# Two token tiles turned on TensorE, two tiles' statistics on ScalarE, and a held weight load

## The chip, the core and the metric

The kernel runs on one core of a Trainium2 chip. The core's engines work side by side and wait for each other through semaphores: TensorE (PE in the profile: matmuls, and its weight loads as PEld), ScalarE (ACT), VectorE (DVE), GpSimd (POOL) and SyncE (SP), which here only issues DMA transfers. The metric is the time of one execution on the device in microseconds (us), smaller is better; the median of three runs before is 1055.08 us (1054.37 to 1055.83).

## The reference

A transformer block with attention and a gated channel MLP, on 2048 tokens of width 1024 in bf16. Normalized tokens `xn` feed both branches:

```python
xn = layernorm(x)                               # x: 1 x 2048 x 1024
# attention, 32 heads of width 32
q, k, v = split(xn @ wqkv)
s = softmax(q @ k.T * 32**-0.5) @ v @ wo
# MLP with its own layernorm, F = 3584
h = gelu(layernorm(xn) @ w1 + b1)
g = silu(h @ w2 + b2)
out = x + s * g
```

(The layout of heads is left out here.) Softmax needs 32 x 2048 x 2048 exponentials, all on ScalarE.

## The kernel before

The kernel is a program that builds a list of operations with their engine, an assumed cost, and what they read and write, lets its own list scheduler (`plan.run`) choose the order for every engine by those assumed costs, and then emits the instructions in that order, with semaphore waits. On the chip each engine runs its list strictly in order. So a changed assumption about a cost moves instructions, though it computes nothing different.

A token tile is 128 tokens x 1024. There are 16 (t = 0 to 15); two of them are a pair n. The opening of the kernel does the following for each tile: load it, take mean and variance, compute the reciprocal root on GpSimd, normalize to bf16 on VectorE (`xnb`, four buffers), turn it so that the width lies on partitions (`xnT`, in `big`), and project K, V and part of Q from it. Tiles below `TD` are turned on TensorE (transposes into PSUM, copied out by ScalarE), the others by a DMA transpose issued from SyncE. Tiles in `AS` have their statistics taken by ScalarE in two passes with an accumulator, the others by VectorE.

```python
XF = 4; QE = 0; AS = (2,); TD = 2; XA = 8; XB = 5; XW = 9
...
for t in range(XF): load_x(t)                   # order of the first loads
wk0 = load_qk(0, 1)
wq0 = load_qk(0, 0)
for t in range(XF, 6): load_x(t)
load_v(0)                                       # wv
for t in range(6, XA): load_x(t)
...
for n in range(NPR):                            # pairs
    for t in (2 * n, 2 * n + 1):
        if t in AS:                             # statistics on ScalarE
            act(activation(junk, xst[t], Copy, scale=-1/32768, accum_out=lnp[:, t, 2:3]))
            act(activation(junk, xst[t], Square, bias=lnp[:, t, 2:3], scale=1/32, accum_out=mv[:, t, 1:2]))
            dve(tensor_scalar_mul(mv[:, t, 0:1], lnp[:, t, 2:3], -32.0))
        else:                                   # statistics on VectorE
            for c in range(2): dve(bn_stats(stats[:, t, c, :], xst[t][:, c * 512:(c + 1) * 512]))
            dve(bn_aggr(mv[:, t, :], stats[:, t]))
        for k in range(XA, NT):                 # later tiles are loaded behind these statistics
            if max(0, k - XB) == t: load_x(k, [("st", t, 0)])
    ...                                         # reciprocal root on GpSimd, then
    xnop[t] = dve(tensor_scalar(xnb[t % 4], xst[t], mean, rstd, subtract, mult))
    for t in (lo, lo + 1):
        if t < TD:
            pro_q.append(tr_item(t))            # 8 TensorE transposes, copy out on ScalarE
        else:
            add("SP", dma_start_transpose(out=xnT[:, :, tile t], in_=xnb[t % 4]), ...)
    pro_q.append(k_pair_item(n, False))         # K of the pair, 8 matmuls of 256
    if n == 1: pro_q.append(q_pair_item(1))     # Q of pair 1
    if n >= VLAG: pro_q.append(v_item(0, n - VLAG, "pro"))   # V, 16 matmuls of 256
```

(Helper arguments, costs and the two tiles of pair 0, which are handled one by one, are cut.) Attention then goes through units: four heads, 256 queries (block qb), 256 keys (pair kp). A unit is eight small score matmuls (two halves of four) and two exponentials of 128 x 1024 on ScalarE, one for each half (line 1181), later the product of the probabilities with V ("PV") on TensorE. The first units alternate between query blocks 0 and 1: (0,0), (0,1), (1,0), (1,1), (0,2), (1,2), (0,3), (1,3) and so on up to pair 7. Units of pair kp can start when K of that pair exists, that is when both its tiles are turned. The exps of this opening are counted from 1 here: 1 and 2 belong to (0,0), 3 and 4 to (0,1), 9 to 12 to the units of pair 2, 13 to 16 to pair 3, 17 to 20 to pair 4, 21 to 24 to pair 5, 25 to 28 to pair 6; 29 is the first of pair 7. While TensorE has nothing to do in the first 32 us of its schedule, "fillers" (matmuls of the identity) are put in.

The weights of the MLP are loaded ahead: `w1` in pieces of 256 KB, the first three pairs of pieces held behind a normalized tile, and `w2` in pieces of 448 KB, not held:

```python
def load_w1(p):
    ...
    dma(f"w1{gi}{i}", ..., [xnop[XW + 2 * p]] if p < 3 else [])
def load_w2(q, r):
    ...
    dma(f"w2{i}", lambda e: e.dma_start(w2r[:, i], src), 580000, [], [("w2", i)])
```

Of the kernel before, what the change touches and what calls it, by code (L numbers as in the profile page):

```python
# [34 lines left out]
XF = 4  # L35
# [5 lines left out]
WLAT = 3300  # L41
# [1 line left out]
NCUT = 2  # L43
HALF = 1
NU = 22
QE = 0
AS = (2,)
FILL = 300
ADJ2 = 0
TD = 2  # L50
XA = 8
XB = 5
XW = 9
ENGS = ("PE", "ACT", "DVE", "POOL", "SP")


# [18 lines left out]
class _Plan:  # L75
# [54 lines left out]
    def run(self, total_units, dense_slack):  # L130
# [28 lines left out]
        def commit(o, t):  # L159
            e = o.eng  # L160
            o.start = t
            if e == "SP":
                if o.prio >= 5:
                    for x in reversed(order["PE"]):
                        if x.fin <= t:
                            o.deps[x] = True
                            break
                tf[e] = t + o.occ
                state["bw"] = max(state["bw"], t) + o.nbytes / 380.0
                o.fin = state["bw"] + {"w1": WLAT, "w2": WLAT, "tp": 2800.0, "x0": 2050.0, "x1": 2000.0, "x2": 2500.0}.get(o.sem[:2], 2300.0)  # L170
            else:
                tf[e] = t + o.occ
                o.fin = t + o.occ + o.lat
            order[e].append(o)
            self.seq.append(o)
            release(o, t)
            wake(tf[e], e)
# [267 lines left out]
        while ev:  # L445
            t, ei = heapq.heappop(ev)
            e = ENGS[ei]
# [109 lines left out]
def bass_recurrent_scan__mha_block__mixer_channel_mlp__prompt_kernel(  # L557
# [39 lines left out]
    with ExitStack() as st:  # L597
# [112 lines left out]
        def pool(fn, occ, R, W, prio=3):  # L710
            return add("POOL", fn, occ, PL, R, W, prio)

        def dma(sem, fn, nbytes, R, W, prio=3, extra=()):
            return add("SP", fn, 430, 0, R, W, prio, sem=sem, nbytes=nbytes, extra=extra)

        def chunk(item, fn, occ, R, mode="f", W=()):
            o = add("PE", lambda e, fn=fn, item=item: fn(e, item.bank), occ, TL, R, W, item=item, mode=mode)
# [36 lines left out]
        def load_v(pr):  # L754
            src = A_wqkv[:, 2 * D + pr * 256: 2 * D + (pr + 1) * 256].rearrange("(c p) n -> p c n", p=128)
            dma("wv", lambda e: e.dma_start(wv, src), 850000, [], [("wv",)])
# [2 lines left out]
            load_x(t)  # L759
        wk0 = load_qk(0, 1)  # L760
        wq0 = load_qk(0, 0)
        for t in range(XF, 6):
            load_x(t)
        load_v(0)
        for t in range(6, XA):
            load_x(t)
        pool(lambda e: e.iota(iota_i, pattern=[[1, 128]], base=0, channel_multiplier=-1), 300, [], [("iota",)])
        dve(lambda e: e.tensor_single_scalar(ident[:], iota_i, 0, op=ALU.is_equal), 220, [("iota",)], [("ident",)], 0)
        dve(lambda e: e.memset(ones[:], 1.0), 90, [], [("ones",)], 0)
# [114 lines left out]
        for n in range(NPR):  # L884
            for t in (2 * n, 2 * n + 1):
                if t in AS:

                    junk = yT[:, 4:8, :].rearrange("p c t -> p (c t)")
                    act(lambda e, t=t: e.activation(junk, xst[t], ACT.Copy, scale=-1.0 / 32768, accum_out=lnp[:, t, 2:3]),
                        c_acts(1024) + 93, [XS(t)], [("yT", 2), ("yT", 3), ("st", t, 0)], 1)  # L890
                    act(lambda e, t=t: e.activation(junk, xst[t], ACT.Square, bias=lnp[:, t, 2:3], scale=1.0 / 32,
                                                    accum_out=mv[:, t, 1:2]),
                        c_acts(1024) + 186, [XS(t), ("st", t, 0)], [("yT", 2), ("yT", 3), ("st", t, 1)], 1)
                    dve(lambda e, t=t: e.tensor_scalar_mul(mv[:, t, 0:1], lnp[:, t, 2:3], -32.0), 65,
                        [("st", t, 0), ("st", t, 1)], [("mv", t)], 1)
                else:
                    for c in range(2):
                        dve(lambda e, t=t, c=c: e.bn_stats(stats[:, t, c, :], xst[t][:, c * 512:(c + 1) * 512]),  # L898
                            600, [XS(t)], [("st", t, c)], 1)
                    dve(lambda e, t=t: e.bn_aggr(mv[:, t, :], stats[:, t, :, :].rearrange("p c s -> p (c s)")),  # L900
                        150, [("st", t, 0), ("st", t, 1)], [("mv", t)], 1)
                for k in range(XA, NT):
                    if max(0, k - XB) == t:
                        load_x(k, [("st", t, 0)])
            lo, hi = 2 * n, 2 * n + 2
            if n == 0:
                for t in (0, 1):
                    dve(lambda e, t=t: e.tensor_scalar_add(lnp[:, t:t + 1, 0], mv[:, t:t + 1, 1], EPS), 90, [("mv", t)], [("ve", 0, t)], 0)
                    pool(lambda e, t=t: e.tensor_tensor(lnp[:, t:t + 1, 1], lnp[:, t:t + 1, 0], mhalf[:, t:t + 1], op=ALU.pow),
                         650, [("ve", 0, t), ("mhalf",)], [("rs", 0, t), ("rs", 0)], 0)  # L910
                    dve(lambda e, t=t: e.tensor_scalar(xnb[t], xst[t], mv[:, t, 0:1], lnp[:, t, 1:2],
                                                       op0=ALU.subtract, op1=ALU.mult), 455,
                        [XS(t), ("mv", t), ("rs", 0, t)], [("xnb", t)], 0.5)
                pro_q += [tr_item(0), qk_tile_item(0), tr_item(1, 0), tr_item(1, 1), qk_tile_item(1)]
                if VLAG == 0:
                    pro_q.append(v_item(0, 0, "pro"))
                continue
            dve(lambda e, lo=lo, hi=hi: e.tensor_scalar_add(lnp[:, lo:hi, 0], mv[:, lo:hi, 1], EPS), 90,
                [("mv", lo), ("mv", lo + 1)], [("ve", n)], 1)
            dve(lambda e, lo=lo, hi=hi: e.tensor_scalar_mul(lnp[:, lo:hi, 4], mv[:, lo:hi, 0], -1.0), 65,  # L920
                [("mv", lo), ("mv", lo + 1)], [("nm", n)], 1)
            pool(lambda e, lo=lo, hi=hi: e.tensor_tensor(lnp[:, lo:hi, 1], lnp[:, lo:hi, 0], mhalf[:, lo:hi], op=ALU.pow),
                 700, [("ve", n), ("mhalf",)], [("rs", n)], 0)
            pool(lambda e, lo=lo, hi=hi: e.tensor_tensor(lnp[:, lo:hi, 5], lnp[:, lo:hi, 4], lnp[:, lo:hi, 1], op=ALU.mult),
                 200, [("nm", n), ("rs", n)], [("nb_", n)], 0)
            for t in (lo, lo + 1):
                if t in DN:
                    xnop[t] = dve(lambda e, t=t: e.tensor_scalar(xnb[t % 4], xst[t], mv[:, t, 0:1], lnp[:, t, 1:2],
                                                                 op0=ALU.subtract, op1=ALU.mult), 455,
                                  [XS(t), ("mv", t), ("rs", n)], [("xnb", t % 4)], 0.5)  # L930
                    continue
                xnop[t] = pool(lambda e, t=t: e.tensor_scalar(xnb[t % 4], xst[t], lnp[:, t, 1:2], lnp[:, t, 5:6],
                                                    op0=ALU.mult, op1=ALU.add), 950,
                     [XS(t), ("nb_", n), ("rs", n)], [("xnb", t % 4)], 1)
            for t in (lo, lo + 1):
                if t < TD:
                    pro_q.append(tr_item(t))
                else:

                    add("SP", lambda e, t=t: e.dma_start_transpose(out=xnT[:, :, t * 128:(t + 1) * 128], in_=xnb[t % 4]),  # L940
                        1290, 0, [("xnb", t % 4)], [("xnT", t, h) for h in range(2)], 0, sem=f"tp{t % 4}", nbytes=262144)
            pro_q.append(k_pair_item(n, False))
            if n == 1:
                pro_q.append(q_pair_item(1))
            if n >= VLAG:
                pro_q.append(v_item(0, n - VLAG, "pro"))
        for n in range(NPR - VLAG, NPR):
            pro_q.append(v_item(0, n, "pro"))
        q_at = len(pro_q)

        pool(lambda e: e.tensor_tensor(lnp[:, :, 2], mv[:, :, 1], lnp[:, :, 1], op=ALU.mult), 150,
             [("rs", n) for n in range(NPR)], [("s2",)], 2)
# [22 lines left out]
        def load_w1(p):  # L975
            gi = p % NW1R
            pi = p % NW1
            for i in range(2):
                src = B_w1[i * 512:(i + 1) * 512, pi * 256:(pi + 1) * 256].rearrange("(c p) f -> p c f", p=128)
                dma(f"w1{gi}{i}", lambda e, i=i, src=src: e.dma_start(w1r[gi][:, 4 * i:4 * i + 4], src), 332000, [], [("w1", gi, i)], 3,  # L980
                    [xnop[XW + 2 * p]] if p < 3 else [])

        def load_w2(q, r):
            i = nw2["n"] % NW2R
            nw2["n"] += 1
            src = B_w2[r * 7 * 128:(r + 1) * 7 * 128, q * 256:(q + 1) * 256].rearrange("(f p) n -> p f n", p=128)
            dma(f"w2{i}", lambda e: e.dma_start(w2r[:, i], src), 580000, [], [("w2", i)])
            return i

        def b1_item():  # L990
# [349 lines left out]

        for tq in range(1, 4):
            it = qk_item(0, 0, tq, wq0, 16 * tq - 12)
            if tq == 1 and QE:
                it.kind, it.due = "pro", 1
                pro_q.insert(q_at - QE, it)
                continue
            plan.queues["proj"].append(it)
            it.after = 1000
# [144 lines left out]
```

The softmax here doesn't subtract the row's maximum and nothing guards it: scores larger than these inputs give would overflow.

## Time and profile before

| | before |
|---|---|
| median of 3 runs | 1055.08 us |
| span of the profiled execution | 1055.5 us |
| TensorE busy | 1028.4 us (97%) |
| ScalarE busy | 1013.0 us (96%) |
| VectorE busy | 960.5 us (91%) |
| exps, 128 x 1024 | 1024, 964.8 us busy |
| DMA transposes | 14 |

A line of the profile's timeline gives start and length in us, the engine, the line of the source, the operation, what it writes and reads, a count of merged instructions, and in brackets how long the engine had been idle before and what ended that. A "q" behind an engine's name is its instruction queue; a DMA is issued there, and its data land later. `gw` and `yT` are the buffers of normalized tiles, `big` the turned tokens, `hT` and `w2r` the raw token tiles before they become hidden values and weights, `qk` projections and their weights, `ut` statistics, `P` probabilities, `ps` PSUM. The chain of waits follows the last instruction back, at each step to what released it.

### The profile page before, as it was taken

The page shows a single profiled execution, that of the slowest core. Times are in us where ns is not written, and L with a number is a line of the kernel's source. Part 1 is how long each engine was busy: PE and PEld are TensorE (multiplying, and loading weights), DVE is VectorE, ACT ScalarE, POOL GpSimd, SP SyncE. Part 2 cuts the span into 40 slices and gives each one's busy share as a digit, 9 for nine tenths or more (in the row PEclk, how much of TensorE's full clock was granted, in tenths as well). Part 3 has the DMA queues.
Part 4 walks back from the last instruction along what each step waited for, and adds up shares of the span by engine and source line. Part 5 has one row for each costly group of instructions (what it writes and reads, how often), then busy time and mean ns, then how long its engine had stood idle before and what let it go on. Part 6 is the DMA issues. An engine that isn't in the chain of part 4 may idle for free.

```text
span 1055.5 us, 32143 instructions
## 1 busy us (share of the span) xinstructions
PE 1028.4 (97%) x14326; PEld 637.6 (60%) x14326; DVE 960.5 (91%) x1454; ACT 1013.0 (96%) x1104; POOL 14.8 (1%) x28
## 2 busy tenths in 40 slices
PE   8899999999999999999999999999999999999997
PEld 4445566656676566656676566656665667664442
DVE  7659999999899999999999999999989999979897
ACT  4699999999999999999999999999999999999993
POOL 1200000000000000000000000000000000000000
PEclk9999999999999999999999999999999999999999
DMA  9945256743276356634465456434475587673431
GB/s 234 186 111 148 79 161 191 197 127 96 70 221 173 108 148 185 173 109 113 117 189 161 113 164 183 141 104 116 143 198 161 171 236 221 205 221 95 137 102 60
DMA packets 302371, 160.16 MB, mean 152 GB/s; under 512 B 40218, under 2 KB 293146, under 8 KB 302234
## 3 DMA queue, kind: packets, MB, share of 16 engines
q1 hardware_dynamic: 302234, 158.12, 53.8%
q8 instruction: 112, 1.84, 0.7%
q14 instruction: 25, 0.20, 0.1%
HBM read 142.35 MB, written 12.06 MB: 146 GB/s over the span
## 4 chain that ended last, share of the span: by engine, by line
ACT 85%; PE 11%; DMA 2%; DVE 1%; SPq 0%; issue 0%; DVEq 0%
ACT P L1181 79%; PE ps L728 7%; ACT ut L1042 5%; PE ps L723 2%; PE ps L1167 2%; ACT gw L1078 1%; DMA big<-gw 1%; DMA big<-yT 1%; DMA hT<-in_A_x_dram 0%; DVE w1r L1328 0%; DVE ut L898 0%; SPq L742 0%; PE ps L866 0%; DVE V L1331 0%; DVE V L1328 0%
## 5 line engine op out<-in xcount | busy, mean ns | idle before, releaser
L1181 ACT ACTIVATE P<-ps 128x1024 bf16<-128x1024 f32 x1024 | 964.8, 1241 | 20.3 <-PE ps L1167 20.2
L1211 DVE TENSOR_TENSOR PA<-P 128x2048 bf16<-128x2048 bf16 x245 | 297.7, 1217 | 17.8 <-ACT P L1181 16.5
L728 PE MATMUL ps<-yT,w1r 128*128 128x256 bf16 x1792 | 232.5, 273 | 0.6 <-DVE yT L1010 0.6
L728 PE MATMUL ps<-w2r,hT 128*128 128x256 bf16 x1792 | 225.0, 273 | 1.8 <-DVE xb L1027 0.6
L728 PEld LDWEIGHTS ps<-yT,w1r 128*128 128x128 bf16 x1792 | 162.7, 98 | 56.2 <-issue 30.6
L728 PEld LDWEIGHTS ps<-w2r,hT 128*128 128x128 bf16 x1792 | 163.8, 98 | 50.8 <-issue 29.6
L723 PE MATMUL ps<-P,V 128*32 128x256 bf16 x4096 | 144.7, 274 | 1.2 <-DVE xb L1027 0.7
L728 PE MATMUL ps<-big,qk 128*128 128x512 bf16 (+2 forms) x568 | 133.4, 361 | 6.1 <-DMA big<-gw 3.8
L1216 DVE TENSOR_TENSOR PA<-PA 128x1024 bf16<-128x1024 bf16 x201 | 135.6, 681 | 1.2
L728 PE MATMUL ps<-qk,big 128*128 128x256 bf16 (+1 forms) x736 | 128.0, 308 | 0.9 <-DMA qk<-in_A_wqkv_dram 0.8
L723 PEld LDWEIGHTS ps<-P,V 128*32 128x32 bf16 x4096 | 97.2, 96 | 34.2 <-issue 23.6
L1167 PE MATMUL ps<-qk 32*128 32x256 bf16 x2048 | 108.6, 274 | 6.0 <-ACT P L1181 5.4
L1167 PE MATMUL ps<-QKT 32*128 32x256 bf16 x2048 | 101.7, 273 | 1.4 <-ACT P L1181 1.2
L728 PEld LDWEIGHTS ps<-qk,big 128*128 128x128 bf16 x736 | 65.2, 98 | 44.8 <-issue 19.2
L1027 DVE TENSOR_TENSOR xb<-ps,b1T 128x512 bf16<-128x512 f32 x112 | 76.4, 684 | 8.4 <-PE ps L728 7.1
L728 PEld LDWEIGHTS ps<-big,qk 128*128 128x128 bf16 x568 | 47.8, 98 | 57.4 <-issue 17.3
L1167 PEld LDWEIGHTS ps<-qk 32*128 32x128 bf16 x2048 | 32.2, 92 | 75.6 <-ACT P L1181 69.0
L1167 PEld LDWEIGHTS ps<-QKT 32*128 32x128 bf16 x2048 | 30.3, 92 | 70.9 <-ACT P L1181 67.8
L1042 ACT ACTIVATE ut<-ut 128x1024 f32<-128x1024 f32 x56 | 71.8, 1282 | 0.0
L1045 DVE SCALAR_TENSOR_TENSOR hT<-ut,xb 128x1024 bf16<-128x1024 f32 x56 | 67.9, 1212 | 1.3 <-ACT ut L1042 0.8
L1040 DVE SCALAR_TENSOR_TENSOR ut<-hT,xb 128x1024 f32<-128x1024 bf16 x56 | 67.9, 1215 | 0.0
L1261 DVE STREAM_TRANSPOSE nt<-ps 128x256 f32<-128x256 f32 x64 | 28.6, 446 | 22.8 <-PE ps L723 22.6
(82 smaller groups left out, 539.6 us busy)
## 6 DMA issues: line engine op xcount, KB each, us to landing
w1r<-in_B_w_dram SPq DMA_DIRECT2D x224, 256.0 KB, 3.5
w2r<-in_B_w_dram SPq DMA_DIRECT2D x128, 448.0 KB, 4.4
qk<-in_A_wqkv_dram SPq DMA_DIRECT2D x16, 256.0 KB, 3.2
g_scratch<-gw SPq DMA_DIRECT2D x32, 128.0 KB, 3.1
o_scratch<-ot SPq DMA_DIRECT2D x56, 64.0 KB, 3.1
big<-o_scratch SPq DMA_DIRECT2D x28, 128.0 KB, 3.7
hT<-in_A_x_dram SPq DMA_DIRECT2D x10, 256.0 KB, 5.3
qk<-in_A_wqkv_dram SPq DMA_DIRECT2D x4, 512.0 KB, 3.7
```

Of the source, the lines that this page charges most:

```text
L723: ins = e.matmul(dst(j), lhsT=lhsT(j), rhs=rhs(j), start=start, stop=stop, tile_position=(0, 32 * j), skip_group_check=True)
L728: return e.matmul(dst, lhsT=lhsT, rhs=rhs, start=start, stop=stop, skip_group_check=True)
L1027: dve(lambda e: e.tensor_tensor(xb_t[i2][:, p % 2].rearrange("p (k t) -> p k t", k=2), bank(it.bank).rearrange("p (k t) -> p k t", k=2), b ...
L1040: dve(lambda e, r=r: e.scalar_tensor_tensor(ut_t[i2][:, r], h[:, r], 1.0 / GA, xb[:, r], op0=ALU.add, op1=ALU.mult), c_f32(r.stop - r.star ...
L1042: act(lambda e: e.activation(ut_t[i2][:], ut_t[i2][:], ACT.Tanh, scale=GC * GA), c_acts(1024), [("ut", i2, 0), ("ut", i2, 1)], [("ut", i2, ...
L1045: dve(lambda e, r=r: e.scalar_tensor_tensor(h[:, r], ut_t[i2][:, r], 1.0, xb[:, r], op0=ALU.add, op1=ALU.mult), c_f32(r.stop - r.start), [ ...
L1078: act(lambda e: e.activation(zh, z, ACT.Tanh, scale=0.5), c_acts(1024), [("z", 0), ("z", 1)], [("zh",)], 1)
L1167: ins = e.matmul(bank(b0[j], kk * 256, (kk + 1) * 256), lhsT=QKT[sl][32 * j:32 * j + 32, 1, kb * 128:(kb + 1) * 128], rhs=QKT[sl][32 * j:3 ...
L1181: x = act(lambda e, h=h: e.activation(P[pi][:, 2 * h:2 * h + 2].rearrange("p j k q -> p (j k q)"), ps[:, pr[h] * 1024:(pr[h] + 1) * 1024], ...
L1211: add2.append(dve(lambda e, p0=p0, a0=a0: e.tensor_tensor(PA_all[:, a0:a0 + 2].rearrange("p u j q -> p (u j) q"), P_all[:, p0:p0 + 2, :, 0 ...
L1216: add4.append(dve(lambda e, a0=a0: e.tensor_tensor(PA[a0], PA[a0], PA[a0 + 1], op=ALU.add), c_b16(1024), [("PA", a0 + 1)], [("PA", a0)], P ...
L1261: a = dve(lambda e: e.transpose(nt_t[i][:], bank(pv.bank, 256, 512)), 368, [], [("nt", i)], 1, pv)
```

## The change

It moves work in the opening. Tiles 2 and 3 are turned on TensorE rather than by DMA transposes (`TD = 4`), and ScalarE takes the statistics of tile 3 beside those of tile 2 (`AS = (2, 3)`). All `w2` loads wait for the normalization of tile 13; the hold of the first `w1` pieces gets an upper bound. The Q projection of tiles 4 to 7 is put at another place in the queue of the opening (`QE`). The scheduler's assumptions on DMA issue cost and time to landing are refined, which reorders instructions. `WVT = 6` writes the place of the wv load as a parameter, with the same place as before. The aim is to let the exponentials start earlier and with fewer gaps.

```diff
-QE = 0
-AS = (2,)
+QE = 5
+AS = (2, 3)
-TD = 2
+TD = 4
+WVT = 6
@@ scheduler: assumed landing of a DMA
-                o.fin = state["bw"] + {"w1": WLAT, "w2": WLAT, "tp": 2800.0, "x0": 2050.0, "x1": 2000.0, "x2": 2500.0}.get(o.sem[:2], 2300.0)
+                o.fin = state["bw"] + {"w1": WLAT, "w2": WLAT, "tp": 2700.0, "x0": 2050.0, "x1": 2000.0, "x2": 2800.0,
+                                           "wv": 3000.0}.get(o.sem[:2], 2500.0)
+                if o.sem == "x3":
+                    o.fin += 900.0
@@ assumed issue cost
-            return add("SP", fn, 430, 0, R, W, prio, sem=sem, nbytes=nbytes, extra=extra)
+            t_dma[0] += 1
+            return add("SP", fn, 430 if t_dma[0] < 9 else 620, 0, R, W, prio, sem=sem, nbytes=nbytes, extra=extra)
@@ DMA transpose: assumed bytes
-                        1290, 0, [("xnb", t % 4)], ..., sem=f"tp{t % 4}", nbytes=262144)
+                        1290, 0, [("xnb", t % 4)], ..., sem=f"tp{t % 4}", nbytes=330000)
@@ place of the Q projection of tiles 4 to 7
+            if n == QE:
+                q_at = len(pro_q)
...
-            if tq == 1 and QE:
-                it.kind, it.due = "pro", 1
-                pro_q.insert(q_at - QE, it)
+            if tq == 1:
+                it.kind, it.due = "pro", 0.5
+                pro_q.insert(q_at, it)
@@ load_w1
-                    [xnop[XW + 2 * p]] if p < 3 else [])
+                    [xnop[min(XW + 2 * p, NT - 1)]] if p < 3 else [])
@@ load_w2
-            dma(f"w2{i}", lambda e: e.dma_start(w2r[:, i], src), 580000, [], [("w2", i)])
+            dma(f"w2{i}", lambda e: e.dma_start(w2r[:, i], src), 580000, [], [("w2", i)], 3, [xnop[min(XW + 4, NT - 1)]])
```

(The hunk that rewrites the loop around `load_v` with the same order is cut.)

More of the change, by code (lines that the diff above doesn't have):

```diff
@@ L711, in pool @@
             return add("POOL", fn, occ, PL, R, W, prio)
+        t_dma = [0]
         def dma(sem, fn, nbytes, R, W, prio=3, extra=()):
-            return add("SP", fn, 430, 0, R, W, prio, sem=sem, nbytes=nbytes, extra=extra)
+            t_dma[0] += 1
+            return add("SP", fn, 430 if t_dma[0] < 9 else 620, 0, R, W, prio, sem=sem, nbytes=nbytes, extra=extra)
         def chunk(item, fn, occ, R, mode="f", W=()):
@@ L761, in bass_recurrent_scan__mha_block__mixer_channel_mlp__prompt_kernel @@
         wq0 = load_qk(0, 0)
-        for t in range(XF, 6):
+        for t in range(XF, XA):
+            if t == WVT:
+                load_v(0)
             load_x(t)
-        load_v(0)
-        for t in range(6, XA):
-            load_x(t)
+        if WVT >= XA:
+            load_v(0)
         pool(lambda e: e.iota(iota_i, pattern=[[1, 128]], base=0, channel_multiplier=-1), 300, [], [("iota",)])
@@ L940, in bass_recurrent_scan__mha_block__mixer_channel_mlp__prompt_kernel @@
                     add("SP", lambda e, t=t: e.dma_start_transpose(out=xnT[:, :, t * 128:(t + 1) * 128], in_=xnb[t % 4]),
-                        1290, 0, [("xnb", t % 4)], [("xnT", t, h) for h in range(2)], 0, sem=f"tp{t % 4}", nbytes=262144)
+                        1290, 0, [("xnb", t % 4)], [("xnT", t, h) for h in range(2)], 0, sem=f"tp{t % 4}", nbytes=330000)
             pro_q.append(k_pair_item(n, False))
@@ L948, in bass_recurrent_scan__mha_block__mixer_channel_mlp__prompt_kernel @@
             pro_q.append(v_item(0, n, "pro"))
-        q_at = len(pro_q)
         pool(lambda e: e.tensor_tensor(lnp[:, :, 2], mv[:, :, 1], lnp[:, :, 1], op=ALU.mult), 150,
```

## The prediction

> **What bounds the kernel now.** I read the page first: TensorE 97%, ScalarE 96%, VectorE 91% busy leave no bound to be named from shares. The view of busy time by windows tells when each was busy.
>
> ```profile
> 40.00:45.00 5.00, 5.00 (x89) 3.32 (x85) 2.53 (x8) 3.08 (x4) 3.53 (x6) 1.00 1.30 205
> 45.00:50.00 5.00, 2.17 (x15) 0.90 (x16) 0.48 (x2) 2.17 (x3) 1.38 (x1) 0.84 0.88 187
> 50.00:55.00 5.00, 5.00 (x49) 2.07 (x52) 1.12 (x2) 2.58 (x4) 0.00 (x0) 0.50 0.70 203
> 55.00:60.00 5.00, 5.00 (x69) 3.00 (x65) 1.12 (x2) 4.27 (x5) 0.00 (x0) 0.98 1.05 272
> 60.00:65.00 5.00, 5.00 (x83) 2.50 (x71) 0.69 (x1) 5.00 (x7) 0.00 (x0) 1.00 0.31 68
> ```
>
> Columns: busy time of TensorE, its weight loads, VectorE, ScalarE and GpSimd, then the granted TensorE clock, DMA share and GB/s. ScalarE is full only from 60 us. From 45 to 55 us TensorE stands still and then runs at a clock of 0.50. The list of waits of ScalarE from 58 us to the end has one row:
>
> ```profile
> ACT P L1181 <- PE ps L1167: 0.6, 1, 0.6
> ```
>
> So after 58 us ScalarE never starves: it runs dense until its last exp ends at 1039.2, and a tail of 16 us follows. In that stretch each engine waits for another one's instructions, not for the clock on the wall. What decides the end is when ScalarE goes dense. I therefore read its timeline up to there.
>
> ```profile
> 14.64 1.94 ACT L1181 ACTIVATE P<-ps 128x1024 bf16<-128x1024 f32 x2 [3.41 <-PE ps L1167]
> 22.09 5.61 ACT L1181 ACTIVATE P<-ps 128x1024 bf16<-128x1024 f32 x6 [5.51 <-PE ps L1167]
> 28.31 3.77 ACT L1181 ACTIVATE P<-ps 128x1024 bf16<-128x1024 f32 x4 [0.62 <-PE ps L1167]
> 32.32 3.81 ACT L1181 ACTIVATE P<-ps 128x1024 bf16<-128x1024 f32 x4 [0.24 <-PE ps L1167]
> 38.66 3.77 ACT L1181 ACTIVATE P<-ps 128x1024 bf16<-128x1024 f32 x4 [2.53 <-PE ps L1167]
> 44.35 1.94 ACT L1181 ACTIVATE P<-ps 128x1024 bf16<-128x1024 f32 x2 [1.92 <-PE ps L1167]
> 49.11 1.02 ACT L1181 ACTIVATE P<-ps 128x1024 bf16<-128x1024 f32 x1 [2.83 <-PE ps L1167]
> ...
> 58.30 32.35 ACT L1181 ACTIVATE P<-ps 128x1024 bf16<-128x1024 f32 x35 [0.56 <-PE ps L1167]
> ```
>
> Exp 1 starts at 14.64, exp 29 at 58.30; the brackets between them, with the four left out (0.48, 0.48, 1.46, 0.17), add to 16.8 us idle. The chain of waits names what TensorE itself waited for:
>
> ```profile
> 13.02 6.74 DMA big<-yT
> ...
> 31.19 5.03 DMA big<-gw
> ...
> 42.39 5.48 DMA big<-gw
> ```
>
> Start and length: three DMA transposes of normalized tiles (3, 9 and 13) hold TensorE until 19.76, 36.22 and 47.87. The queue's timeline shows what was in flight before the third:
>
> ```profile
> 37.85 1.13 SPq L980 DMA_DIRECT2D w1r<-in_B_w_dram  x2
> 39.02 0.52 SPq L987 DMA_DIRECT2D w2r<-in_B_w_dram  x1
> 40.32 6.93 SPq L940 DMA_TRANSPOSE big<-gw  x3
> ```
>
> **What the Trainium skill says.** "TensorE: Matmul & The Clock Gate", part 1 (the HAM clock gate): a window of about 3.4 us with TensorE idle halves its clock, a busy one restores it. The trace agrees: windows cut at 45.0, 48.4, 51.8 and 55.2 show 0.56 us of TensorE work in the first and a clock of 0.50 in the next two. "DMA: Bandwidth & Descriptors", "Issuing engines are not separate DMA queues": all transfers share 16 DMA engines and interleave. Here a transpose lands 2.7 us after issue at best, tile 12's takes 6.6 us behind w1 and w2 (the w2 piece alone 7.0). "ScalarE: Activation LUTs", "What ACT_TABLE_LOAD costs": 186 ns + 0.833 per element, 93 more for a pointer operand. For 1024 that is 1039 and 1132 ns; the two statistics passes took 1056 and 1148. The first page's part 4 (PE-mode transpose): a TensorE transpose lands in PSUM and must be copied out; here eight take 0.62 us and the copy of a tile 1.02.
>
> **The change part by part.** In the program as built, TensorE and VectorE have before's order again from the scores of exp 21 on, but for one w1 matmul moved late, and ScalarE differs by the added work alone. The queue also moves some late loads. So the whole gain is the shift of exp 29.
>
> Removed: two DMA transposes (1.35 and 3.25 us of queue time, 5.7 and 6.7 us to landing), two VectorE statistics of tile 3 (1.2 us), and one w2 load of 448 KB ahead of the last four transposes. The new bound on w1 equals the old (9, 11, 13 are all below 15): only w2 is held, on tile 13. Added on ScalarE: two passes for tile 3 (1.2 us each, from row starts 6.34 and 7.53) and two copies (1.0 each), 4.4 us; on TensorE 16 transposes (1.2 us), against 4 fewer fillers.
>
> I step through, with durations from the timeline, in the new order.
>
> Exp 1. Pass one of tile 3 runs 8.8 to 9.95 and pushes tile 0's copy from 9.72 to about 9.97. The Q/K matmuls of tiles 0 and 1 then start at 11.0 instead of 10.80. But the scores now stand ahead of the V matmuls that waited for the wv load until 13.77. Evacuation ends 13.5, exp 1 at 14.0 (before 14.64). Pass two falls into the idle time before it.
>
> Exp 3. VectorE finds tile 3's mean at 13.45, GpSimd the power (0.7 us) by 14.45; tile 6's statistics stand ahead, so tiles 2 and 3 are normalized at about 16.1 and 16.6. TensorE turns them by 17.3, ScalarE copies by 18.7, K and Q of the pair (16 matmuls, 1.9 us with the pipeline) end at 20.7. Exp 3 at 21.1 instead of 22.09. Turning on TensorE saves only 1 us here, since statistics and two copies stand in the place of the DMA.
>
> Exps 9 and 13. With no transposes of tiles 2 and 3 in its way the queue issues tile 4's at 17.3 (18.82), tile 6's near 23.5 (24.72), tile 8's near 27.5 (29.90), tile 9's near 28.7 (31.19). VectorE's freed 1.2 us helps. The 0.62 and 0.24 us idle vanish: exp 9 at 26.7, exp 13 at 30.6.
>
> Exp 17. Tile 9's transpose still has w1's first pieces right behind it, so I keep its 5.0 us: landing 33.7 (36.21). Now TensorE is the bound. From that landing to exp 21's scores the new order holds K matmuls (0.88), 5 half scores (1.6), Q of 5 x 512 (1.08), 128 PV matmuls (3.95) and K and V of the next pair (1.73), or 9.2 us, against 7.65 before (36.26 to 43.91), when Q and one half score stood ahead of the wait. Exp 17 at 36.5, exp 21 at 43.2 (44.35).
>
> Exp 29. Exp 21's scores start at 42.9; two halves and 6 V matmuls later (1.3 us), at 44.2, TensorE needs tile 13's transpose. VectorE normalizes tiles 12 and 13 near 38.8 and 39.3 (39.76, 40.2); with only w1's second pieces in flight and no w2, I put the landing at 43 to 44. Then the wait of 2.83 us goes, TensorE keeps its clock, and exps 21 to 28 follow each other at 0.935 (six took 5.61): 43.2 + 7.5 = 50.7, so exp 29 at 50.9, allowing 0.2.
>
> Shift: 58.30 - 50.9 = 7.4 us. Of it about 1.2 is there by exp 21; 6.2 is the third wait and the slow clock: ScalarE's idle brackets from 49.11 to 58.30 (2.83 + 0.48 + 0.48 + 1.46 + 0.17 + 0.56 = 5.98), and the excess of four lone exps (1.02 each). Each wait that I set to zero may come back in part, so I take 6.3 of the 7.4: 1055.1 - 6.3 = 1048.8.
>
> **The rivals.**
> 1. Tile 13 lands late all the same (46 to 47): w1's second pieces took 4.6 us too, and the engines were full. For it speaks a DMA share of 0.9 to 1.3 from 30 to 45 us. Then exp 29 comes near 53 or 54, gain 4 to 5; with a window long enough for the half clock only 1 to 2: 1053 to 1054.
> 2. Tile 9's landing takes less than 5 us. Then TensorE starts its 9.2 us stretch at 32 and the shift grows to 8.5, where tile 13 limits it: 1046.5.
> 3. The passes and copies on ScalarE delay the exps. They lie in gaps of 3.4 and 5.5 us, so this costs about 0.2 us; were all 4.4 us paid, the gain would be 2: 1053.
> 4. The held w2 or weights behind it come late. TensorE's list of waits after 60 us has no DMA in it, so there is room; I give it no time.
>
> **Range and chances.** Rivals 1 and 2 set 1046.5 to 1052.5. 2% is 21 us, more than all of ScalarE's idle time between exps 1 and 29, so within 2% is nearly certain: faster by over 2% 0.01, within 0.98, slower by over 2% 0.01.
>
> **What would show it.** Exp 1, 3, 17, 21 and 29 near 14.0, 21.1, 36.5, 43.2 and 50.9; no clock of 0.50 between 45 and 56; tile 13's transpose landing before 44.5; ScalarE without waits after exp 29, and a span shorter by just the shift of exp 29. I am wrong if exp 29 moves and the end does not, or if the slow clock stays.

## The result and the profile after

| | before | after |
|---|---|---|
| median | 1055.45 us (4 runs, 1054.37 to 1059.37) | 1049.33 us (4 runs, 1047.82 to 1050.10) |
| span of the profiled execution | 1055.5 us | 1048.1 us |
| exp 21, exp 29 start | 44.35, 58.30 | 41.98, 50.11 |
| from exp 29 to the end | 997.2 | 998.0 |

The ratio is 0.9934 (95% interval 0.9905 to 0.9962). A repeat beside other kernels gave 1049.32 us (7 runs) and 0.9941 (0.9920 to 0.9962).

ScalarE's timeline of the changed kernel (same columns as before; its exps are now at line 1190, its copies of turned tiles at 885):

```profile
13.50 1.94 ACT L1190 ACTIVATE P<-ps 128x1024 bf16<-128x1024 f32 x2 [1.42 <-PE ps L1176]
16.05 1.94 ACT L885 ACTIVATE big<-ps 128x1024 bf16<-128x1024 bf16 x2 [0.62 <-PE ps L874]
20.33 9.27 ACT L1190 ACTIVATE P<-ps 128x1024 bf16<-128x1024 f32 x10 [2.34 <-PE ps L1176]
30.05 2.86 ACT L1190 ACTIVATE P<-ps 128x1024 bf16<-128x1024 f32 x3 [0.45 <-PE ps L1176]
33.48 1.02 ACT L1190 ACTIVATE P<-ps 128x1024 bf16<-128x1024 f32 x1 [0.56 <-PE ps L1176]
35.42 3.77 ACT L1190 ACTIVATE P<-ps 128x1024 bf16<-128x1024 f32 x4 [0.92 <-PE ps L1176]
41.98 7.62 ACT L1190 ACTIVATE P<-ps 128x1024 bf16<-128x1024 f32 x8 [2.79 <-PE ps L1176]
50.11 32.35 ACT L1190 ACTIVATE P<-ps 128x1024 bf16<-128x1024 f32 x35 [0.51 <-PE ps L1176]
```

The row at 41.98 is the change in one line: exps 21 to 28 are one run of eight in 7.62 us, where before had six pieces spread over nearly 14 us. The busy time by windows (TensorE, its loads, VectorE, ScalarE, GpSimd, clock, DMA share, GB/s) shows TensorE without a gap and the clock at 1.00 from 45 to 55 us:

```profile
45.00:50.00 5.00, 5.00 (x75) 2.74 (x72) 0.95 (x2) 4.53 (x5) 0.00 (x0) 1.00 0.89 208
50.00:55.00 5.00, 5.00 (x75) 2.84 (x71) 0.69 (x1) 4.89 (x6) 0.00 (x0) 1.00 1.12 296
```

The chain of waits in the opening has one transpose left where before had three. Ahead of it stands VectorE with statistics (`ut`), normalizations (`gw`) and the copy of V out of PSUM (`V`):

```profile
24.65 1.19 DVE ut L906 x2
25.84 0.45 DVE gw L936
26.29 0.60 DVE V L806
26.89 0.46 DVE gw L936
...
27.60 4.86 DMA big<-gw
```

That is tile 9, landing at 32.45. Tile 13 lands at 42.35, before TensorE asks for it. And the list of ScalarE's waits after 52 us has a row that before did not have at that place:

```profile
ACT P L1190 <- PE ps L1176: 1.0, 1, 1.0
```

It lies at 927 us and is explained below.

### The profile page after: what moved, and what is told of

The parts are those of the page before. It is cut to its first block, busy times and chain, and to the rows that moved or that the text cites. A ratio compares the mean times of both kernels' runs of the same rounds, so it can differ in the third digit from the quotient of the medians.

```text
span 1048.1 us, 32171 instructions
## 1 busy us (share of the span) xinstructions
PE 1024.4 (98%) x14338; PEld 637.1 (61%) x14338; DVE 959.5 (92%) x1452; ACT 1016.8 (97%) x1110; POOL 14.8 (1%) x28
## 4 chain that ended last, share of the span: by engine, by line
ACT 83%; PE 12%; DVE 2%; DMA 2%; SPq 1%; issue 0%; DVEq 0%
ACT P L1190 77%; PE ps L735 7%; ACT ut L1051 5%; PE ps L730 2%; PE ps L1176 2%; ACT gw L1087 1%; DVE ut L906 1%; DMA hT<-in_A_x_dram 1%; DMA w2r<-in_B_w_dram 1%; DMA big<-gw 0%; SPq L749 0%; DVE gw L936 0%; DVE w1r L1337 0%; DVE V L806 0%; SPq L757 0%; DVE qk L834 0%
```

## The experiments

Exp 29 minus exp 21 tells the third wait and what follows it, free of how early an execution's opening was; eight dense exps would be 7.5. "Full clock" counts the runs whose mean TensorE clock was 0.998 or more; the four low runs that were profiled (before, e6, e8, e11) show a stretch at 0.50 of 6.8 or 13.7 us behind the third wait, and of the others only the mean is known. The edits are against the kernel in brackets.

| run (edited from) | median us (runs) | ratio to before, 95% | full clock | exp 21 | exp 29 | difference |
|---|---|---|---|---|---|---|
| before, profiled once | | | | 44.35 | 58.30 | 13.95 |
| changed kernel | 1049.33 (4) | 0.9905 to 0.9962 | 4 of 4 | 41.98 | 50.11 | 8.13 |
| e1 hold alone (before) | 1050.04 (6) | 0.9930 to 0.9968 | 6 of 6 | 42.20 | 51.04 | 8.84 |
| e2 no hold (changed) | 1051.18 (9) | 0.9936 to 0.9967 | 9 of 9 | 41.61 | 50.42 | 8.81 |
| e3 w1 later (changed) | 1048.44 (6) | 0.9916 to 0.9951 | 6 of 6 | 41.40 | 49.53 | 8.13 |
| e4 fetch moved (changed) | 1048.70 (6) | 0.9920 to 0.9955 | 6 of 6 | 41.28 | 50.03 | 8.75 |
| e5 warm gap (before) | 1053.02 (22) | 0.9966 to 0.9990 | 22 of 22 | 42.23 | 53.20 | 10.97 |
| e6 before, fetch moved (before) | 1056.45 (22) | 1.0002 to 1.0031 | 0 of 22 | 45.41 | 63.07 | 17.66 |
| e7 TD back (changed) | 1057.90 (22) | 1.0015 to 1.0048 | 12 of 22 | | | |
| e8 costs only (before) | 1057.13 (14) | 0.9984 to 1.0020 | 2 of 14 | 42.64 | 59.33 | 16.69 |
| e9 clear (changed) | 1048.68 (6) | 0.9911 to 0.9959 | 6 of 6 | 41.16 | 49.35 | 8.19 |
| e10 changed again | 1049.32 (7) | 0.9920 to 0.9962 | 7 of 7 | 42.02 | 50.35 | 8.33 |
| e11 before, 21 split (before) | 1056.08 (14) | 0.9996 to 1.0028 | 1 of 14 | 42.82 | 56.66 | 13.84 |
| e12 AS back (changed) | 1049.85 (14) | 0.9933 to 0.9962 | 13 of 14 | 41.32 | 50.66 | 9.34 |

Positions and differences are from one profiled execution each. Those of before, e6 and e8 lie 1.9, 6.1 and 2.5 us above the medians of their kernels, that of e5 0.8 below.

Beside these runs the kernel before was executed 109 times. 21 executions had the full clock, median 1052.31 us; 88 had less, median 1056.03.

**The hold alone.** The kernel before, one line changed; TensorE, VectorE and ScalarE keep their order.

```diff
-            dma(f"w2{i}", ..., 580000, [], [("w2", i)])
+            dma(f"w2{i}", ..., 580000, [], [("w2", i)], 3, [xnop[13]])
```

> The kernel before with one edit: all w2 loads wait for the normalization of tile 13. Tiles 2 and 3, statistics and order on TensorE, VectorE and ScalarE stay as before. Two theories of the third wait of before (tile 13's transpose landed at 47.87 us, TensorE waited, then its clock fell to 0.50). Backlog: the w2 piece stood in front of the transposes; then without it tile 13 lands by 44 to 45, the clock stays at 1.0, exp 29 comes at 52.5 to 53 instead of 58.3, and the time falls by about 5.5 us. Fetch: the DMA rate falls to nearly nothing for about 2 us whenever a 16 KB instruction fetch of TensorE's stream meets transposes in flight, which in before happens at 42.7; that fetch stays where it is, so tile 13 lands at 46 or later, TensorE still waits 1.3 us or more, and the time falls by 4 us at most.

Measured: 5.9 us below before (1055.97 beside it). ScalarE's timeline from exp 21 on:

```profile
42.20 1.94 ACT L1181 ACTIVATE P<-ps 128x1024 bf16<-128x1024 f32 x2 [1.92 <-PE ps L1167]
44.53 2.85 ACT L1181 ACTIVATE P<-ps 128x1024 bf16<-128x1024 f32 x3 [0.40 <-PE ps L1167]
47.67 2.86 ACT L1181 ACTIVATE P<-ps 128x1024 bf16<-128x1024 f32 x3 [0.29 <-PE ps L1167]
51.04 32.35 ACT L1181 ACTIVATE P<-ps 128x1024 bf16<-128x1024 f32 x35 [0.51 <-PE ps L1167]
```

The gap of 2.83 is 0.40, and no exp stands alone any more. TensorE's own list of waits between 40 and 52 us, in before and with the hold alone:

```profile
PE ps L728 <- DMA big<-gw: 2.8, 1, 2.8
```

```profile
PE ps L728 <- DMA big<-gw: 0.6, 1, 0.6
```

Tile 13's transpose took 4.06 us instead of 5.48, tile 12's 4.38 instead of 6.64. So the w2 piece in front was worth 1.4 to 2.3 us of landing, and TensorE's wait was 2.8 us with it and 0.6 without; only with 2.8 did the clock fall. The backlog theory holds for the time. That tile 13 landed at 43.5 and not at 46 is no verdict against the fetch theory, because this execution's opening was 2 us earlier than the profiled one of before: exp 21 at 42.20 with the same order.

**The changed kernel without the hold.**

```diff
-            dma(f"w2{i}", ..., 3, [xnop[min(XW + 4, NT - 1)]])
+            dma(f"w2{i}", ...)
```

> The changed kernel with w2 not held (as before). Backlog: 448 KB more in front of the transposes of tiles 12 and 13, so tile 13 lands 2 to 3 us later than its 42.35, at about 45; TensorE waits 1 to 2 us before exp 29; time 1.5 us above the changed kernel's, and 4 to 5 us above if the wait is long enough to bring the clock of 0.50 back. Fetch: in the changed kernel the fetch falls at 37.7, before those transposes are issued, so they stay fast: landing by 43.5, exp 29 within 0.5 us of 50.1, time as the changed kernel's.

Between the two expectations: tile 13 landed at 42.88, TensorE waited 0.6 us, and the median is 1.9 us above the changed kernel's, with a spread of 1049.14 to 1052.98 (the intervals in the table overlap). No run lost its full clock. So there are two ways to get rid of the third wait's worst, the hold and the rest of the change, and each does most of it alone; their gains do not add. The fetch part of the expectation fell: it came at 39.0, not 37.7, and fell among the transposes.

**The scheduler's assumptions alone**, on the kernel before: the new costs and the new place of the Q projection, with `TD = 2`, `AS = (2,)` and no hold.

```diff
-QE = 0
+QE = 5
+WVT = 6
...    # new landing and issue costs, as in the change
```

> The kernel before with the scheduler's new assumptions and the new place of the Q projection alone: no hold of w2, tiles 2 and 3 by DMA, ScalarE takes tile 2 alone. If it is the new order that keeps the third wait away without the hold, the clock is 0.998 or more in all runs and the median is 1051 to 1052. If the two transposes fewer on the queue do it, the third wait and the half clock are back in most runs: 1054.5 to 1056.

The third wait is back, and the clock falls in 12 of 14 runs:

```profile
42.64 1.94 ACT L1190 ACTIVATE P<-ps 128x1024 bf16<-128x1024 f32 x2 [1.91 <-PE ps L1176]
47.82 1.02 ACT L1190 ACTIVATE P<-ps 128x1024 bf16<-128x1024 f32 x1 [3.24 <-PE ps L1176]
49.32 1.02 ACT L1190 ACTIVATE P<-ps 128x1024 bf16<-128x1024 f32 x1 [0.48 <-PE ps L1176]
```

So the new order is not what protects the kernel without the hold; what differs between this run and the one before it is where tiles 2 and 3 are turned and their statistics taken (and what the scheduler makes of it). There tile 13's transpose was issued 3.0 us before exp 21 (38.60 against 41.61), here 1.8 (40.83 against 42.64). VectorE has only a small part in that: it begins to normalize tile 12 4.88 us before exp 21 there (36.73) and 4.59 here (38.05). The rest lies on the queue. There tile 13's issue follows tile 12's after 1.3 us, here after 2.2, and the w2 piece is issued 2.0 us ahead of tile 12's transpose there, 1.3 here. Which of these counts was not taken apart.

**What the clock costs.** The kernel before with work for TensorE during the third wait; it removes nothing.

```diff
+warm = add("PE", ...)   # 12 x full(bank of K of pair 6, ident, ident x 4), ahead of its first K matmul;
+                        # it has the waits of that matmul except the one on the transposes
```

> The kernel before with twelve extra 128 x 512 matmuls of the identity on TensorE (2.6 us at full clock) right ahead of the K matmuls of tiles 12 and 13, where TensorE waits for tile 13's transpose; nothing else is changed, the transposes least of all. If the half clock is most of what the third wait costs: the wait stays (exp 25 still follows a gap of 2 to 3 us), the clock stays at 1.0 and exps 25 to 28 follow densely, so exp 29 comes near 54.5 in an execution whose tile 13 lands at 47.9; every run has a mean clock of 0.998 or 0.999, and the median is about 1052.3, as in the two runs of before that kept the clock (1052.22, 1052.30). Rival: the wait itself costs and the clock does not; then the median stays above 1055.

```profile
42.23 1.94 ACT L1184 ACTIVATE P<-ps 128x1024 bf16<-128x1024 f32 x2 [1.92 <-PE ps L1170]
46.69 2.86 ACT L1184 ACTIVATE P<-ps 128x1024 bf16<-128x1024 f32 x3 [2.52 <-PE ps L1170]
49.84 2.86 ACT L1184 ACTIVATE P<-ps 128x1024 bf16<-128x1024 f32 x3 [0.29 <-PE ps L1170]
53.20 32.35 ACT L1184 ACTIVATE P<-ps 128x1024 bf16<-128x1024 f32 x35 [0.51 <-PE ps L1170]
```

The wait is there (2.52) and the exps behind it are dense: all 22 runs at full clock, 2.8 us below before. The part from exp 21 to 29 falls from 13.95 to 10.97. From exp 23, the first behind the wait, to exp 29 it falls from 9.19 to 6.51, and the hold alone has the same 6.51: so about 2.7 us are the clock. The wait itself is the other half: from 10.97 to 8.84 with the hold. The 109 executions of before point the same way without any edit: 3.7 us between those that kept the clock and those that did not, though the former may have waited less as well.

**TensorE's turn of tiles 2 and 3 undone.**

```diff
-TD = 4
+TD = 2
```

> The changed kernel with TD = 2: tiles 2 and 3 are turned by DMA transposes as before, w2 stays held, ScalarE still takes the statistics of tile 3. If turning tiles 2 and 3 on TensorE gives about 1 us of exp 3's start and that 1 us lasts, the median is 1 us above the changed kernel's: 1050 to 1050.8, as with the hold alone (1050.04). Rival: the opening is set by loads and normalizations, and the exps from 9 on come at the same time with either; then 1049.0 to 1049.6.

Both theories missed, by 7 and 8 us. ScalarE is dense from 50 us, as early as in the changed kernel, and then starves:

```profile
50.00 15.91 ACT L1190 ACTIVATE P<-ps 128x1024 bf16<-128x1024 f32 x17 [0.17 <-PE ps L1176]
71.65 1.94 ACT L1190 ACTIVATE P<-ps 128x1024 bf16<-128x1024 f32 x2 [5.74 <-PE ps L1176]
```

With another number of transposes the scheduler makes another order: ahead of the scores for the exp at 71.65 it sets K, Q and PV matmuls, and TensorE then waits 1.04 us for VectorE's first output normalization. So this run does not measure the turning of two tiles, it measures another schedule. What `TD = 4` is worth in time by itself stays open; a run that keeps the order of the rest was not tried. Only exp 3 can be read (below).

**Statistics of tile 3 back on VectorE.**

```diff
-AS = (2, 3)
+AS = (2,)
```

> The changed kernel with the statistics of tile 3 back on VectorE; tiles 2 and 3 are still turned on TensorE and w2 is held. VectorE has 1.2 us more in the opening, ScalarE 2.4 us less. If VectorE's chain of statistics and normalizations sets the opening, as the chain of waits of the changed kernel shows from 13.6 to 27.5 us, the transposes of tiles 4 to 9 come up to 1.2 us later and the median is 0.5 to 1.2 us above the changed kernel's. Rival: ScalarE's passes were in the way; then the time is the same or lower.

Median 0.5 us above the changed kernel beside it, the low end of the first theory, but its runs lie between 1048.01 and 1052.70 and the intervals overlap: not settled. In the opening the passes were in the way: VectorE normalizes tile 3 at 12.10 instead of 15.26, exp 3 comes at 18.09 rather than 20.33 and exp 21 at 41.32 rather than 41.98. The order behind that differs too: tile 12's transpose takes 5.71 us, TensorE waits 1.2 us for tile 13's, and the lead is gone by exp 29 (50.66). Exp 3 in three runs, each with the new costs of the scheduler (e7, e8 and this one; e8 has no hold of w2, which acts later); the changed kernel has it at 20.33:

```profile
22.13 6.64 ACT L1190 ACTIVATE P<-ps 128x1024 bf16<-128x1024 f32 x7 [6.62 <-PE ps L1176]
20.17 5.81 ACT L1190 ACTIVATE P<-ps 128x1024 bf16<-128x1024 f32 x6 [5.82 <-PE ps L1176]
18.09 5.61 ACT L1190 ACTIVATE P<-ps 128x1024 bf16<-128x1024 f32 x6 [1.75 <-PE ps L1176]
```

| exp 3 | tile 3's statistics on VectorE | on ScalarE |
|---|---|---|
| tiles 2 and 3 by DMA | 20.17 (e8) | 22.13 (e7) |
| tiles 2 and 3 on TensorE | 18.09 (e12) | 20.33 (changed kernel) |

So the turn on TensorE brings exp 3 about 2 us forward, and the passes on ScalarE take about 2 us away again; each number is from one profile, with the order that the scheduler made for it.

**Tile 9's transpose: w1 behind it, or something else?** Two edits of the changed kernel, one for each suspect.

```diff
-XW = 9
+XW = 11          # e3: first w1 pieces behind tile 11, not 9; w2 behind tile 15
```

```diff
-full(e, bank(b), ident, ident x 4)                                        # 128 x 512
+[full(e, bank(b, 128*i, 128*i + 128), ident, ident) for i in range(4)]    # e4: the same work, 4 instructions
```

> The changed kernel with the three held pairs of w1 pieces held behind tiles 11, 13 and 15 rather than 9, 11 and 13 (w2 behind tile 15). Tiles 8 and 9 then have no weights behind them in the queue. If w1's first pieces are what makes tile 9's transpose take 4.86 us (landing 32.45), it now takes about 2.8 and lands near 30.4, the exps from 17 on come up to 2 us earlier. If it is the instruction fetch at 29.06, nothing changes up to exp 21: tile 9 lands at 32.2 to 32.6. The later pieces may now collide with tiles 12 and 13: then exp 29 comes late by 1 us or so.

> The changed kernel with every filler and warming matmul of the identity (128 x 512) written as four of 128 x 128: the same work and order, but some 150 more TensorE instructions ahead of the opening's transposes, so TensorE's instruction fetches come at other times: the one at 29.06 goes to about 21, the one at 37.7 to about 33. Fetch: tiles 8 and 9 land without the stall, tile 9 near 30.4 instead of 32.45, exps 17 and 21 come 1 to 2 us earlier, though the fetch near 33 may meet the transposes of tiles 10 and 11. Rival (w1 or the transposes' own traffic makes tile 9 late): landing and exps stay within 0.4 us of the changed kernel's.

Durations of the transposes of tiles 8 and 9, from issue to landing. e6 and e11 are runs of the kernel before that are described below; they bear on this question too:

| | fetch among them | no fetch among them |
|---|---|---|
| w1 behind them | 5.26, 4.86 (changed kernel); tile 9: 5.03 (before), 4.82 (e1) | 3.94, 3.76 (e4); tile 9: 2.83 (e6), 2.81 (e11) |
| no w1 | 4.73, 4.13 (e3); 4.43 (tile 8 in e9, below) | 3.03 (tile 9 in e9) |

The fetch is the cause of most of it. In the order of before, w1 is issued 1.35 us behind tile 9's transpose each time, and that takes 4.8 to 5.0 us with a fetch and 2.8 without one. w1 behind it costs nothing there; beside a fetch it may add 0.5 to 0.7 (the changed kernel against e3). e4's 3.94 and 3.76 have another reason at hand: a token tile's load of 256 KB was issued 0.6 us ahead of tile 8's transpose; that was not tested. The DMA rate (last number) shows the fetch: the windows of the changed kernel, and the queues of the window 29 to 30 us, where the instruction fetch is the only packet that moves:

```profile
28.00:29.00 1.00, 1.00 (x12) 0.72 (x12) 0.75 (x4) 1.00 (x2) 0.00 (x0) 1.00 3.78 190
29.00:30.00 1.00, 1.00 (x16) 0.54 (x14) 1.00 (x4) 0.60 (x1) 0.46 (x1) 1.00 0.06 16
30.00:31.00 1.00, 1.00 (x11) 0.58 (x7) 1.00 (x3) 0.94 (x2) 0.43 (x2) 1.00 0.31 57
```

```profile
DMA packets 1, 0.02 MB, mean 16 GB/s; under 512 B 0, under 2 KB 0, under 8 KB 0
q8 instruction: 1, 0.02, 6.0%
```

And the same windows with the fetch moved away:

```profile
28.00:29.00 1.00, 1.00 (x12) 0.54 (x10) 0.55 (x2) 0.82 (x2) 0.00 (x0) 1.00 1.13 320
29.00:30.00 1.00, 1.00 (x13) 0.72 (x15) 0.75 (x4) 0.74 (x1) 0.17 (x1) 1.00 1.13 248
30.00:31.00 1.00, 0.95 (x13) 0.63 (x14) 1.00 (x3) 0.66 (x1) 0.72 (x2) 1.00 1.15 203
```

The hole is gone here; a new one of 0.9 us stands at 40.3, behind the fetch that now comes at 39.4. In time neither edit is shown to gain: 1048.44 and 1048.70, ranges overlapping the changed kernel's 1047.82 to 1050.10.

**Both edits, and a smaller shift.** XW = 11, and only the first seven identity matmuls split.

```diff
-XW = 9
+XW = 11
-for _ in range(WARM): chunk(it, ident 128 x 512)
+for j in range(WARM): chunk(it, 4 x ident 128 x 128 if j < 7 else ident 128 x 512)
```

> The changed kernel with w1's pieces held behind tiles 11, 13 and 15 as in the run with w1 later, and the first seven identity matmuls of 128 x 512 written as four of 128 x 128, so that TensorE's instruction fetches come 42 instructions earlier: near 27, 36.5 and 46, each at a time without transposes in flight. If w1 and the fetch are together what made tiles 8 and 9 take 5.26 and 4.86 us: both now take 2.7 to 3.0, tile 9 lands at 30.5, exp 17 comes at 33.5, exp 21 at 40.1, exp 29 between 48.2 and 48.8, and the median is about 1047.3. Rival: something else holds those transposes; then tile 9 lands at 31.5 or later and the time is that of the run with w1 later.

The first part missed. Tile 9's transpose took the 3.0 us expected, but was issued 1 us late, because tile 8's held the queue for 2.29 us: the fetch came at 26.4, not 27, took 1.69 us, and packets stood from 28.1 to 29.3. So the landing was 31.64, not 30.5. Exp 29 came at 49.35, 1.0 earlier than in the changed kernel run beside it, and the median is 0.6 lower (1048.68 to 1049.32, intervals overlapping). None of the versions is shown to beat the change.

**The changed kernel again**, without an edit.

> The changed kernel as it is, run beside the others: a median of 1049 to 1049.7, a mean clock of 0.998 or 0.999 in every run; exp 29 between 49.5 and 50.5; the profile shows which of its times vary from one execution to the next.

As expected. Its exp 21 is within 0.04 us of the first profile's, and it has no wait at 927 us.

**Is the fetch a cause of the third wait as well?** The kernel before with all identity matmuls split (e6), and with the first 21 (e11).

```diff
-full(e, bank(b), ident, ident x 4)
+4 x 128 x 128                       # e6: all
+4 x 128 x 128 if n <= 21, else 128 x 512   # e11, n counts them in TensorE's order
```

> The kernel before with each identity matmul of 128 x 512 written as four of 128 x 128: w2 is still ahead of the last transposes, but TensorE's instruction fetch of 42.7 comes some 6 us earlier, near 36, before tile 12's transpose is issued. Fetch: tile 13 lands within 4.5 us of its issue instead of 5.48, TensorE's wait is about 1 us shorter, the half clock is gone in most runs, and the median is 1051.5 to 1053. Backlog: tile 13's transpose still takes 5.5 us, the clock is 0.996 or less in most runs, and the median stays at 1055 to 1056.

> The kernel before with only the first 21 identity matmuls written as four (126 instructions more, not 174): TensorE's third fetch moves from 42.7 to about 39.7, ahead of the transposes of tiles 12 and 13, and the fourth to after the third wait, which the run with all of them moved into that wait. w2 stays in front. If w2 and the fetch each add their part (from the runs so far: without both 3.2 and 2.8 us for tiles 12 and 13, with the fetch alone 4.4 and 4.1, with both 6.6 and 5.5): they now take 5.4 and 4.2, TensorE's wait before exp 23 is 1.2 us shorter than in before, and more runs than 1 in 5 keep the clock. If the fetch is no cause of its own: 6.6 and 5.5 again.

Both missed their aim for the third wait. The fetch of 42.7 moved (to 38.1 and 37.9, where it met tiles 10 and 11), but the next one came forward with it, to 46.4 and 43.3, among the transposes of tiles 12 and 13 again. These took 7.50 and 5.71 us, and 6.62 and 4.91. In no run does w2 stand in front of them without a fetch, so the fetch's part in the third wait is not separated; that w2 has one is shown by the hold alone.

## Why the prediction was right, and where it was not

Time and range were right, and so was the mechanism that carried the number: exps 21 to 28 dense, no half clock, nothing to do with VectorE or the busy shares.

**What ends the kernel.** The claim that the gain is exp 29's shift held in every run but e7: from exp 29 to the end took 996.9 to 998.5 us, whatever the kernel.

**The third wait and the clock, 6.2 us of the 7.4.** Confirmed at 5.8 (13.95 to 8.13), and split: about 3 us clock (13.95 to 10.97; 2.7 if counted from exp 23), 2.1 us wait (10.97 to 8.84), with 0.5 to 0.7 more in the changed kernel; each from one profile. Predicted difference from exp 21 to 29 was 7.7, measured 8.13 and 8.33. Tile 13 landed at 42.35 (said 43 to 44), tile 9 at 32.45 (33.7). The TensorE stretch after it was sized well: 9.53 us from that landing to exp 21, against 9.5 (33.7 to 43.2). The 5.0 us kept for tile 9's transpose were right (4.86) for a wrong reason, which is luck: not w1 behind it, but a fetch, which fell among the transposes in the changed kernel as it had in before.

**The opening, 1.2 us by exp 21.** This term was wrong. The profiles show even 2.4 (44.35 to 41.98), but two more executions with before's order up to there give exp 1 at 13.21 and 12.91, exp 3 at 20.15 and 20.09, exp 21 at 42.20 and 42.23, against 13.50, 20.33 and 41.98. So what the two profiles differ by in the opening is nearly all one late execution of before: its wv load landed at 13.72, that of the hold alone at 11.78. Tiles 2 and 3 on TensorE and tile 3's statistics on ScalarE together gain nothing at exp 3, where they pull against each other (table above), and the 1.6 us that tile 9 gains on the hold alone (34.06) is eaten by the longer stretch behind it (9.53 against 8.14). The step's stretch was right; its landing of before, 36.21, was that execution's.

**What was booked, 6.3 of 7.4.** Exp 29 moved by 8.2, more than said, the span by 7.4, the median by 6.1. The rest is two things. The profiled executions lay above their medians, that of before by 1.9 us (1057.32), that of the changed kernel by 0.6 (1049.94). And 0.8 was lost late. That 6.3 came so near to 6.1 is in part luck: the 1.1 us taken off for waits that might come back stands, unnamed, for the 1.2 of the opening that is not there.

**Rival 4, the late weights, got no time and cost about 1 us in most profiles.** ScalarE and TensorE of the changed kernel near the end:

```profile
927.20 1.94 ACT L1190 ACTIVATE P<-ps 128x1024 bf16<-128x1024 f32 x2 [1.01 <-PE ps L1176]
```

```profile
925.23 1.59 PE L735 MATMUL ps<-w2r,hT 128*128 128x256 bf16 x13 [1.33 <-DMA w2r<-in_B_w_dram]
```

TensorE waits for a w2 piece. Of eight profiles with the new order of late loads (e7 left out) six have this wait at ScalarE, 0.6 to 1.4 us; the five with before's order have none. It is there without the hold too (e2, e8), so the hold is not its cause. Nor does the order look like it: from 863 to 958 us the queue issues transfers between the same buffers in the same order as with the hold alone, which has no wait. What differs is when an instruction fetch comes. In the six profiles with the wait the piece took 4.96 to 5.57 us to land, and a fetch began between 0.3 us before and 3.3 us after its issue. In six of the other seven it took 4.02 to 4.27, and a fetch began 3.6 us after the issue or later, or not at all; the seventh (e11) has a fetch and 5.14 us, but no wait. The two profiles of the changed kernel fall on both sides: 5.30 and a fetch 1.9 us after the issue, 4.27 and 3.7 in its second profile. No run moved that fetch on purpose, so this is a coincidence in 13 profiles and not an experiment. The prediction saw no DMA in one list of waits of before and took that for room; in that execution the fetch came 3.7 us after the issue.

**Rivals 1 to 3.** Tile 13 was not late (w1's second pieces were through). Tile 9's landing stayed near 5 us; where it was shortened (e3, e4, e9), 1048.4 to 1048.7 came out, not 1046.5. ScalarE's passes cost about 2 us at exp 3 and 0.7 by exp 21 beside e12 (the prediction had about 0.2 for passes and copies), but no cost in time is shown (1049.32 against 1049.85 without tile 3's).

## What to carry to other kernels

Hold back a load that nobody needs soon when it stands in front of transfers that TensorE waits for: one line of dependency by itself gave 5.9 us, the whole change 6.1. Look for a wait just long enough to cost the clock, since here it was paid about twice; the mean clock of each run, beside its time, shows how often. And compare parts of two profiles only after a second execution of the same order: a difference in the opening of 2 us was the execution, not the change.

## What was not expected of the hardware

**Where an instruction fetch meets transposes in flight, they stop.** TensorE's instructions come in pieces of 16384 bytes on a queue of their own, about one for every 256 of its instructions, as the Trainium skill says ("Runtime: NRT & Kernel Launch", "Instruction fetch mechanics"); it calls the cost "mostly hidden". The trace agrees on the number: 112 such pieces for 28652 matmuls and weight loads in the profile of before. TensorE does not wait in the one case shown (the changed kernel has a fetch at 47.45, and TensorE is busy 5.00 of 5.00 us from 45 to 50), but the DMA queue does. Counting only time in which a transpose had been outstanding for 1.3 us or more, the 14 profiles have 35 stretches of 0.75 to 2.25 us under 40 GB/s in the first 52 us. Each begins between 0.5 us before and 2.0 us after the record of an instruction fetch starts (30 times one of TensorE's 16 KB, 5 times one of 8 KB on another queue), though such surroundings of fetches make up only 0.29 of the time counted. When the fetches were moved, the stretches moved. How the one stops the other no view shows. Transposes alone on the queue moved at 288 GB/s in before (46.0 to 47.2 us).

**The half clock is a matter of the execution.** The kernel before, whose profile shows TensorE waiting 2.8 us for tile 13, lost its full clock in 88 of 109 executions; the two kernels whose profiles show 0.6 us there (e1, e2) kept it in 15 of 15. The wait of 2.8 us is shorter than the window of 3.4 us that the prediction speaks of, and that window was not wholly idle: it held 0.56 us of TensorE work when the clock was lost.
